# Four lower halves of an exponential table: from a product on VectorE to an exponential on ScalarE, in a new order

## The chip, the cores and the metric

The kernel runs on one core of a Trainium2 chip. The metric is the time of one execution on the device in microseconds (us), as the median of several runs. In all that follows PE is TensorE, PEld its weight loads, DVE is VectorE, ACT is ScalarE, POOL is GpSimd and SP is SyncE, which issues most of the DMAs.

## The reference

Two branches over the same input x (2048 positions, 512 channels) are mixed by a gate:

```python
g = _sigmoid((x * gate_w).sum(-1, keepdims=True))
a = _A_ref(x, ...)          # long convolution of each channel
b = _B_ref(x, wqkv, w_phi, wo)  # linear attention, 32 heads of 16
return g * a + (1 - g) * b
```

Branch A builds, for each channel d, a filter of 2048 lags from 128 complex states, and convolves by FFT:

```python
logdA = dt * A
P = jnp.exp(logdA[:, :, None] * l[None, None, :])
K = jnp.einsum("dn,dnl,dn->dl", Cc, P, dB).real
```

Branch B has features softmax(q w_phi) and softmax(-q w_phi), likewise for k, and divides num by den.

## The kernel before

**Units.** The 512 channels are cut into 16 units U of 32 channels; four units make a quarter Q. The filter of a unit is a sum over the 128 states (the partitions) of a coarse table A (32 steps of 64 lags) times a fine table R (64 lags). `plan_tables` makes the cosines and sines `cs` of the fine table (two Sin activations a unit), `plan_exp` its magnitudes `E`, `kgen` the rest. DVE makes A in two products A1, A2 (L1116, L1121), and for units whose digit in `FOURS` is 0 a sum A3 (L1126). It makes R in two products: `Rh` (L1133) from E's upper half and `Rl` (L1137) from E's lower half with `cs` read backwards. PE sums A times R into `kps`, which is copied out as `KD`.

**E.** A product of `statE` and `selE` on PE puts the 32x32 arguments of a unit (decay rate times lag t + 1/2, with t from 0 to 31) into a PSUM tile `args`. ACT's Exp gives the upper half, `E[:, 1]`. The lower half, `E[:, 0]`, has lags from -31.5 to -0.5. It is the upper half times exp(-32 x rate), kept in `Gtab`; DVE does that product, node `El`, L1063:

```python
nc.vector.tensor_tensor(out=T.E[:, 0]..., in0=T.E[:, 1]...,
                        in1=g.G[:, 32 * U:32 * U + 32].unsqueeze(2).to_broadcast([128, 32, 16, 2]), op=ALU.mult)
```

**Transforms.** `KD` goes through PE's stage `psA` (copied out as XA) and `psB` (copied out as XK, L143 on ACT, L145 on DVE). DVE multiplies XK by the input's transform, loaded as `XUX` (or into Dtab), giving `t` (L1251, and L1254 for the units 14 and 15). PE's `psz` turns back (copied out as Zr). For quarters 0 to 2 Zr goes to DRAM (`Zd`) and returns turned as `ZT`; for quarter 3 DVE turns it in place (L1337). PE's `psy` adds the attention to it, and DVE multiplies by the gate into xT (L1388, L1391). Units 14 and 15 go through this alone, unit 15 in halves.

**Attention.** Keys come first, up to about 75 us. Queries come in four blocks. In each, ACT exponentiates `pq` into Eq, `zs` sums it, and a short chain runs to and fro: ACT Ln (`zs`, `den`), DVE (L887 to L889), ACT Ln (`den`), DVE (L895), ACT Exp (`apm`). SP writes `apm` to DRAM (`apd`, L909) and reads it back spread over the partitions as `ax` (L916). DVE multiplies Eq by `ax` (L923, twice a block), then PE's `ops` makes the output, copied out as oT. There is one buffer for `ax`, which ZT uses too. The last block is the late one; its scaled copies are at L991 (ACT) and L993 (DVE), and the copies `Ctab<-psy` hold what the other quarters give it.

**Order.** Nothing is scheduled at run time. Every step is a node, `ORDER` lists all nodes in the order of issue, and each engine works off its own nodes in that order. `SIDES` says for each eviction whether ACT or DVE does it, `RINGS` which of two PSUM rings a tile comes from (each ring has two tiles of two banks), and `WARM` puts extra matmuls ahead of some. An engine whose next instruction waits holds up all that is behind it, SP's queue of DMAs included.

Of the kernel before, what the change touches and what calls it, by code (L numbers as in the profile page):

```python
# [10 lines left out]
ACT = mybir.ActivationFunctionType  # L11
# [58 lines left out]
class Plan:  # L70

    DIGITS = "0123456789abcdefghijklmnopqrstuvwxyzABCDEFGHIJKLMNOPQRSTUVWXYZ-_"
    ORDER = ("0H0J0B0C0D100L001112130y0z0A0102030j0k0l0m0n0o0d0e0f0g0h0i0405060s0t0u0a0b0c0708090p0q0r180I0T0U0V0W0K0M0X0O0P0Z0Q0R0Y0-0N14"
             "2u2w2x2v152Q2S2R2T2U2W16191a2V2Y2-2Z1x2_2y2z0S0_17342X1v2A1b1d1m1e1n1y1f1z2B2K2I2L1G2J301w3231331o1H1I0v0w0x2E2C2G2D2O2F1K2P"
             "1J1M1B1A35361D2H371E1c1p1q1r1g1h1i0E0F0G2M383a2N1C394B4I4K4J4L3c4X3d3b1F4P4Z4Y4-4M4_3e4T3g1X4N4U4Q4O4R4V52564S4W3h1Q571S3f5a"
             "5c3i53503j5b511T54585d5h4C5e554D593k3m5l1Y1U5i3l5f1L5g3n5m3Q5n5j5p5r5q5s3o3q3p3r5w5A5B1N5t5k5o3v3x5E3R5u5v5x5y5C1R5G5L3w3S5F"
             "5H5z5P3y5M1O4E1P3s3t3u3z3A3B3C3E5D5T5I5J5K5U5V5W5X5Q5N3D5R3F1V5-5O623J3L5S5Y3T5_3K5Z636064666768696a3U3V6d61656l6n3M6e3W3Y6m"
             "6o6p6b3G3H3I1s1t1u3N3O3P3X6q6c3Z6r3-3_6h406i6f426s41441W1Z1-261_436t20226j28456w4647486g4a2749294b2a6x2c6y2b216u232d2e2n244c"
             "4d4e4f4h6k6v4i4g4m4o2f2o4p4n2g6z2p4j4k4l2h2i2j2k2l254t4v4w2q4F2r2s2m4u4q4r4s4x4y4z1j1k1l2t4A8y6A6E9j9k9l6B6C6D9d9e9f8z8A6F8j"
             "6H8l8n8k8p8m8o8q8r4G8v8w4H9g9h9i6G6I8x8B8C6J8E8F8G8K8L6L8S7c8D6K6M6N8T7e7gag6O7d7hah8H8I8J6P8U8Y6Q7f6R8Z8M8N7i7L6S7j6T6U6V8s"  # L80
             "8t8u6W6X6Y6-6_708O8_907N7k8Q8P7l8V8W95918X7m7O7M7n8R96ai7o8-7Pap7R7Qaq7pa6aaab92936Zar94717q7r7s7t7u7v7x7y7z9798a7aca972aeam"
             "ajanak737wavawal999b749aa89cadaf7S76aoaD7T78aE9p7U77asat7A7V799q757W9r7XaFaJauaxay9xaM7B7D9yaN7Y9z9s9A7E9t7C9BaKc7c89FbZ7Z7-"
             "7_b1b2b38081828485869u9v9w9C9D9E9m9n9oaOaGaH9GaSaIc983879HaTc1c27Fb_7Gc47H9N9OazaB88aAaC897IaLc0c58a7Jb-8c8b7Kc3c68e7a8daPaQ"
             "cd9Pce8faRaU7baV8gcgaW8hch8icacbcccmcicn9IcDaXcE9QaY9JaZ9Ra-a_b0eEeFeGcRcScTeBeCeD9S9T9U9K9L9M9V9W9Xcfbacubbcvd-bie0d_bjcFcj"
             "ckcwclcJcKbcbke1eNcobdbleOcpbebme2bqbycAcBcxcye3bzbre4cz9_eWe5eXa0cqcse6a1cre7b4b5b6b7b8b99Y9Z9-bfbgbhe8e9eabnbobpdQcCcta2a3"
             "dRdUdVdWbsbAcGcHeYa4cIePeTeUa5cLcMbtbudScNcPbBcOcQd1d9cXcYcZebecedefegehcUcVcWbvbwbxbCbDbEbFd2eQeReeeid3f0daeSdbejeVekdXdhdi"
             "d4dpdqdcdTd5dddYdZeKeLeMbGbHbIc-c_d0bJbKbLf1eZe-dje_drd6d7d8dedfdgeHeIeJbMbNfmdkf2bOdsdlfndtdmdndoelf3embPfHbQf4f6fIdDfpfqfo"
             "fsftbRfrf7bSf5fuf8fvfbfwf9fxfcdudvdwdxdydzdAdBdCfJfNfOfKfLfMdEdGdHdIfafddFfyfzfAdJfPfQfRfSfTfUenfVfefheofWepfffifXfYfZfBfgfj"
             "f-f_fCg0fDg2eqg1fEg3dNdOdPdKdLdMbWbXbYbTbUbVereseteufkeyezeAevewexflfFfGg4g5g6g7g8g9gagb")
    SIDES = ("01110001001001010000000011000101001010000000110110000000100001100110010101011010000000000100000000000100000000000000"  # L90
             "0000000000000000000000000000100010000000000100000010110")
    RINGS = ("00001011111110101110000000000000000000101000000000000000001001000010000000101101000111110010111111011110001110101000"
             "00011001")
    WARM = ("01000000000001000050000200004000010000300000000060000004030050000010005000060100000040000310600000001000000030000000"
             "10000000000000000000100")
    FOURS = ("0111110101011000")
    ZPS = ("00000001")

    HOT = ("pk", "vp", "pq", "zp", "ops", "bps4", "psA", "psBu", "psB128", "psB64", "psB32", "psz", "pszn", "psyn32", "psy128", "psy64", "psy32", "kps")
# [47 lines left out]
    def run(self):  # L147
        code = {d: i for i, d in enumerate(self.DIGITS)}
        order = [64 * code[a] + code[b] for a, b in zip(self.ORDER[0::2], self.ORDER[1::2])] or list(range(len(self.nodes)))
        assert sorted(order) == list(range(len(self.nodes)))  # L150
        sides, rings, warm = iter(self.SIDES), iter(self.RINGS), iter(self.WARM)
        for n in self.nodes:
# [516 lines left out]
def attention_keys(P, nc, g, psum, r):  # L669
# [40 lines left out]
    for s2 in range(8):  # L710
# [20 lines left out]

        def ps4(K=K, box=box, on=P.ZPS[s2] == "1"):
            if not on:
                return
            box.ps = bank("zk")
            for u in range(2):
                e = K.E[:, u].rearrange("p g (h a b) -> p (g h) a b", a=4, b=4)
                for k in range(4):
                    nc.tensor.matmul(box.ps[:, 256 * u:256 * u + 256], lhsT=g.ident[:], rhs=e[:, :, k, :], start=(k == 0), stop=(k == 3), skip_group_check=True)

        def rd(K=K, box=box, on=P.ZPS[s2] == "1"):
            K.Z = g.kwk.tile([128, 2, 2, 32], F32, name="Zk")
# [302 lines left out]
def plan_exp(P, nc, g, psum, U, T, psq, deps):  # L1045

    act = g.act
    h, cc = U // 2, U % 2
    box = Bag()

    def pe():
        T.E = g.epool.tile([128, 2, 32, 32], BF16, name="E", bufs=g.P.k["E"])
        box.ps = psum([128, 2, 16, 32], "args")
        for e in range(2):
            nc.tensor.matmul(box.ps[:, e], lhsT=g.statE[64 * e:64 * e + 64, h, :], rhs=g.selE[64 * e:64 * e + 64, 16 * cc:16 * cc + 16, :],  # L1055
                             start=True, stop=True, tile_position=(64 * e, 0))

    def ex():
        act(out=T.E[:, 1], in_=box.ps[:].rearrange("p e x t -> p (e x) t"), func=ACT.Exp)
        box.ps = None  # L1060

    def el():
        nc.vector.tensor_tensor(out=T.E[:, 0].rearrange("p c (t k) -> p c t k", k=2), in0=T.E[:, 1].rearrange("p c (t k) -> p c t k", k=2),  # L1063
                                in1=g.G[:, 32 * U:32 * U + 32].unsqueeze(2).to_broadcast([128, 32, 16, 2]), op=ALU.mult)
    a = P.add("PE", "argE", pe, deps, take=[psq, "E"], rw=("stE selE", ""))
    T.nE.append(P.add("ACT", "E", ex, [a], drop=["psum"], tab="L"))
    T.nE.append(P.add("DVE", "El", el, T.nE[-1:], rw=("G", "")))


def plan_conv(P, nc, g, psum, r):  # L1070
# [33 lines left out]
    def kgen(units, XA, new, split=False):  # L1104
        K = Bag()
        K.done, kps, nu = [], [], len(units)
        for cc, U in enumerate(units):
            t = T[U]
            plan_exp(P, nc, g, psum, U, t, psq, [sh])
            four = P.FOURS[U] == "1"  # L1110
            c = Bag()
# [537 lines left out]
```

## Time and profile before

| | |
|---|---|
| runs | 251.51 us median of 3 (250.56 to 252.16) |
| the profiled execution | 251.85 us, its span 250.1 us |
| granted PE clock, mean | 0.977 |
| busy PE, PEld, DVE, ACT, POOL | 204.3, 140.2, 233.5, 222.0, 9.6 us |

The span runs from the first to the last instruction. Busy time of an engine is the sum over its instructions. In a timeline a row gives start, duration, engine, line, operation, tiles and shapes; what stands in brackets at its end is the time for which the engine had nothing running ahead of it, and what ended that. In a row of groups the count is followed by the total busy time, the mean duration in ns, and the idle time ahead.

### The profile page before, as it was taken

The numbers are of one execution on the slowest core, as the hardware profiler recorded it, in microseconds if no ns is written. First come the engines' busy times: TensorE is split into PE (matmuls) and PEld (weight loads), VectorE is DVE, ScalarE is ACT, GpSimd is POOL, SyncE is SP. The second block draws the span as 40 slices with busy tenths as digits, with TensorE's granted clock in tenths as the row PEclk, the third lists the DMA queues.
The fourth block names the chain that finished last, engine by engine and source line by source line (L and its number), as shares of the span: only waits on it lengthen the run. The fifth ranks groups of instructions, "written<-read, shape, count | busy, mean of one in ns | idle before, by whom it ended". The sixth has DMA issues, their size and how long they took to land.

```text
span 250.1 us, 9880 instructions
## 1 busy us (share of the span) xinstructions
PE 204.3 (82%) x4387; PEld 140.2 (56%) x4409; DVE 233.5 (93%) x316; ACT 222.0 (89%) x309; POOL 9.6 (4%) x21
## 2 busy tenths in 40 slices
PE   0687999999955846999897888999988698889980
PEld 0677566555634512556555645855767376677440
DVE  7999999999999999999979999999989799999890
ACT  7999999999999899999999899999989978875540
POOL 4820000000000000000000000000000000000000
PEclk9999999999999797999999999999999999999996
DMA  6998000445503765605350078554655979850645
GB/s 187 202 208 210 17 3 4 128 128 155 144 0 99 229 190 145 229 7 146 111 164 9 5 230 213 181 160 84 223 164 136 265 175 292 202 172 18 127 113 101
DMA packets 52842, 34.86 MB, mean 139 GB/s; under 512 B 30528, under 2 KB 48320, under 8 KB 52800
## 3 DMA queue, kind: packets, MB, share of 16 engines
q1 hardware_dynamic: 51456, 33.78, 51.4%
q8 instruction: 34, 0.56, 1.0%
q10 hardware_dynamic: 1344, 0.46, 0.9%
q14 instruction: 8, 0.07, 0.1%
HBM read 21.38 MB, written 12.58 MB: 136 GB/s over the span
## 4 chain that ended last, share of the span: by engine, by line
PE 29%; DVE 20%; DMA 19%; ACT 16%; issue 8%; SPq 5%; DVEq 0%; ACTq 0%
PE pk L718 5%; DMA ax<-apd 5%; PE vp L766 5%; DMA UD<-in_A_u_dram 4%; ACT cs L67 3%; DVE t L1251 2%; ACT Eq L67 2%; PE psz L1280 2%; PE kps L177 2%; DMA wc<-in_B_w_phi_dram 2%; DMA XUX<-XUd 2%; DVE R L1133 2%; DVE xT L1391 2%; DMA ZT<-Zd 2%; PE pq L852 2%
## 5 line engine op out<-in xcount | busy, mean ns | idle before, releaser
L177 PE MATMUL kps<-R,A 128*32 128x64 bf16 x1600 | 29.4, 229 | 1.8 <-DVE A L1121 1.8
L67 ACT ACTIVATE cs<-args 128x1024 bf16<-128x1024 f32 x32 | 30.7, 1052 | 0.0
L177 PEld LDWEIGHTS <-A 128*32 128x32 bf16 x1600 | 27.3, 161 | 5.7 <-DVE A L1121 2.2
L1116 DVE TENSOR_TENSOR A<-Ctab,Dtab 128x2048 bf16<-128x2048 bf16 x16 | 19.5, 1218 | 0.2 <-PE kps L177 0.2
L1133 DVE TENSOR_TENSOR R<-E,cs 128x2048 bf16<-128x2048 bf16 x16 | 19.5, 1219 | 0.0
L1137 DVE TENSOR_TENSOR R<-E,cs 128x2048 bf16<-128x2048 bf16 x16 | 19.5, 1218 | 0.0
L1121 DVE TENSOR_TENSOR A<-Ctab,Dtab 128x2048 bf16<-128x2048 bf16 x16 | 19.5, 1219 | 0.0
L143 ACT CAST Zr<-psz 128x1024 bf16<-128x1024 f32 (+1 forms) x16 | 16.0, 1026 | 3.7 <-DMA Zd<-Zr 1.9
L143 ACT CAST XA<-psA 128x1024 bf16<-128x1024 f32 (+1 forms) x17 | 16.5, 1005 | 1.6 <-PE psA L184 1.5
L67 ACT ACTIVATE Ek<-pk 128x512 bf16<-128x512 f32 x32 | 16.7, 604 | 0.7 <-PE pk L718 0.6
L67 ACT ACTIVATE E<-args 128x1024 bf16<-128x1024 f32 x16 | 16.9, 1053 | 0.4 <-PE args L1055 0.4
L67 ACT ACTIVATE Eq<-pq 128x512 bf16<-128x512 f32 (+1 forms) x28 | 16.8, 685 | 0.2 <-PE pq L852 0.2
L852 PE MATMUL pq<-xT,Wqp 128*128 128x512 bf16 x64 | 16.3, 386 | 0.4 <-ACT Eq L67 0.4
L745 DVE TENSOR_REDUCE Zk<-Ek 128x64 f32<-128x1024 bf16 x14 | 16.4, 1209 | 0.0
L766 PE MATMUL vp<-WW,xT 128*128 128x512 bf16 x62 | 15.9, 380 | 0.2
L718 PE MATMUL pk<-WW,xT 128*128 128x512 bf16 x58 | 14.5, 379 | 0.6 <-issue 0.5
L1251 DVE TENSOR_TENSOR t<-XUX,XK 128x2048 bf16<-128x2048 bf16 x12 | 14.5, 1219 | 0.3 <-DMA XUX<-XUd 0.3
L143 ACT CAST XK<-psB 128x1024 bf16<-128x1024 f32 (+1 forms) x14 | 13.7, 1000 | 1.0 <-PE psB L190 1.0
L625 PE MATMUL psB<-XAu,TB 64*128 64x128 bf16 x256 | 10.5, 231 | 4.5 <-ACT xst L143 2.5
L143 ACT CAST xst<-psB 128x1024 bf16<-128x1024 f32 x13 | 13.2, 1040 | 0.9 <-DMA XUd<-xst 0.9
L64 ACT ACT_TABLE_LOAD x10 | 12.8, 1283 | 0.9 <-PEq L1633 0.7
L923 DVE TENSOR_TENSOR Eq<-Eq,ax 128x2048 bf16<-128x2048 bf16 x8 | 9.7, 1221 | 4.0 <-DMA ax<-apd 4.0
(215 smaller groups left out, 504.8 us busy)
## 6 DMA issues: line engine op xcount, KB each, us to landing
XUX<-XUd SPq DMA_DIRECT2D x28, 256.0 KB, 4.4
XUd<-xst SPq DMA_DIRECT2D x8, 512.0 KB, 3.0
ax<-apd SPq DMA_DIRECT2D x16, 256.0 KB, 5.0
Zd<-Zr SPq DMA_DIRECT2D x24, 128.0 KB, 4.2
ZT<-Zd SPq DMA_DIRECT2D x6, 512.0 KB, 5.5
UD<-in_A_u_dram SPq DMA_DIRECT2D x16, 128.0 KB, 4.5
XUd<-xst SPq DMA_DIRECT2D x8, 256.0 KB, 3.7
wqk<-in_B_wqkv_dram SPq DMA_DIRECT2D x1, 1024.0 KB, 5.5
```

The costliest lines, as they stand in the source:

```text
L67: return self.nc.scalar.activation(**kw)
L143: self.nc.scalar.copy(out=o, in_=i)
L177: nc.tensor.matmul(kps[32 * dj:32 * dj + 32, g4, e, :], lhsT=A[:, ka, :, :, d].rearrange("p a b -> p (a b)"), rhs=R[:, kr, d, :], start=(i ...
L718: nc.tensor.matmul(box.ps[:], lhsT=xT[:, st, kt, :], rhs=g.WW[:, kt, :], start=(kt == 0), stop=(kt == 3))
L745: nc.vector.tensor_reduce(out=K.Z[:, u].rearrange("p g h -> p (g h)"), in_=K.E[:, u].rearrange("p g (h f) -> p (g h) f", f=16), axis=mybir ...
L766: nc.tensor.matmul(box.ps[:], lhsT=xT[:, st, kt, :], rhs=g.WW[:, 4 + kt, :], start=(kt == 0), stop=(kt == 3))
L852: nc.tensor.matmul(box.ps[:, m - m0, :] if late else box.ps[:], lhsT=g.Wqp[:, kt, 128 * m:128 * m + 128], rhs=xT[:, 4 * b:4 * b + 4, kt, : ...
L1116: nc.vector.tensor_tensor(out=c.A[:, 0:2].rearrange("p o a b c -> p (o a) b c"), in0=g.C[U // 8][:, 0:2, :, d0 % 256:d0 % 256 + 32].rearra ...
L1121: nc.vector.tensor_tensor(out=c.A[:, 2:4].rearrange("p o a b c -> p (o a) b c"), in0=g.C[U // 8][:, 1:3, :, d0 % 256:d0 % 256 + 32].rearra ...
L1133: nc.vector.tensor_tensor(out=c.R[:, :, :, 32:64], in0=t.E[:, 1].unsqueeze(1).to_broadcast([128, 2, 32, 32]), in1=t.cs[:], op=ALU.mult)
L1137: nc.vector.tensor_tensor(out=c.R[:, :, :, 0:32], in0=t.E[:, 0].unsqueeze(1).to_broadcast([128, 2, 32, 32]), in1=t.cs[:, ::-1, :, ::-1], o ...
L1251: nc.vector.tensor_tensor(out=box.t, in0=Ls[r0 // ns].X[:], in1=box.XK[:].unsqueeze(1).to_broadcast([128, 2, 1024]), op=ALU.mult)
```

## The change

For units 12 to 15 (`ELS`) ACT makes the lower half too, from the same PSUM arguments, with the sign turned by `scale=-1` and the lags written backwards; exp(-(t + 1/2) x rate) at the place 31 - t is what the product gave. The PSUM tile is released after the second exponential. DVE's El stays for units 0 to 11. `ORDER`, `SIDES`, `RINGS` and `WARM` are new throughout:

```diff
-    ORDER = ("0H0J0B0C0D100L001112130y0z0A0102030j0k0l0m0n0o0d0e0f0g0h0i0405060s0t0u0a0b0c0708090p0q0r180I0T0U0V0W0K0M0X0O0P0Z0Q0R0Y0-0N14"
...
+    ORDER = ("0H0J0L100B0C0D120y0z0A0d0e0f0j0k0l0m0n0o0405060102030g0h0i0s0t0u0a0b0c0p0q0r070809180I0T0011130X0V0U0Z0W0-0Y0K0M0N2w0O2u142v"
...
     FOURS = ("0111110101011000")
+    ELS = ("0000000000001111")
...
     def ex():
         act(out=T.E[:, 1], in_=box.ps[:].rearrange("p e x t -> p (e x) t"), func=ACT.Exp)
+        if not low:
+            box.ps = None
+
+    low = P.ELS[U] == "1"
+
+    def ela():
+        act(out=T.E[:, 0, :, ::-1], in_=box.ps[:].rearrange("p e x t -> p (e x) t"), func=ACT.Exp, scale=-1.0)
         box.ps = None
...
-    T.nE.append(P.add("ACT", "E", ex, [a], drop=["psum"], tab="L"))
-    T.nE.append(P.add("DVE", "El", el, T.nE[-1:], rw=("G", "")))
+    T.nE.append(P.add("ACT", "E", ex, [a], drop=([] if low else ["psum"]), tab="L"))
+    if low:
+        T.nE.append(P.add("ACT", "El", ela, [T.nE[-1], a], drop=["psum"], tab="L"))
+    else:
+        T.nE.append(P.add("DVE", "El", el, T.nE[-1:], rw=("G", "")))
```

The lines behind move: L1063 becomes L1071, and what stands behind plan_exp moves by 11, the copies by 1. Evictions change sides: counted over the order, after unit 0's first product DVE gets two casts of Ctab, two of oT, one large one of KD, a half of Zr, one scale (L993) and two casts of 256 columns (KD and xT), and gives up one large XK, one half XK and one cast of oT into wo. Ahead of it DVE gets one xst and one wT and gives up one XAu and one WW. ACT has the opposite of each.

Three places of the order. The first is on DVE, between the first and the second query block's Eq. Before:

```order
L923 TENSOR_TENSOR Eq<-Eq,ax 128x2048
L1133 TENSOR_TENSOR R<-E,cs 128x64x32
L1116 TENSOR_TENSOR A<-Ctab_75,Dtab 128x2048
L1137 TENSOR_TENSOR R<-E,cs 128x64x32
L1121 TENSOR_TENSOR A<-Ctab_75,Dtab 128x2048
L145 CAST wo<-ops 128x512
L923 TENSOR_TENSOR Eq<-Eq,ax 128x2048
L1133 TENSOR_TENSOR R<-E,cs 128x64x32
```

and in the change:

```order
L924 TENSOR_TENSOR Eq<-Eq,ax 128x2048 x2
L1127 TENSOR_TENSOR A<-Ctab_75,Dtab 128x2048
L1132 TENSOR_TENSOR A<-Ctab_75,Dtab 128x2048
L1144 TENSOR_TENSOR R<-E,cs 128x64x32
L146 CAST wo<-ops 128x512
L1148 TENSOR_TENSOR R<-E,cs 128x64x32
L1144 TENSOR_TENSOR R<-E,cs 128x64x32
L1148 TENSOR_TENSOR R<-E,cs 128x64x32
L924 TENSOR_TENSOR Eq<-Eq,ax 128x2048 x2
```

Six large operations and a cast stand between the blocks instead of four and a cast, and the two halves of a block follow each other at once. The second place is on ACT, in the last query block, from `zs` to `apm`. Before:

```order
L67 ACTIVATE zs<-zs 128x256
L67 ACTIVATE den<-zs 128x256
L143 CAST XK<-psB 128x1024 x2
L67 ACTIVATE den<-den,eps 128x128
L67 ACTIVATE E<-args 128x1024
L143 CAST XA<-psA 128x32x32
L67 ACTIVATE apm<-zs 128x256
```

and in the change:

```order
L67 ACTIVATE zs<-zs 128x256
L67 ACTIVATE den<-zs 128x256
L67 ACTIVATE E<-args 128x1024
L67 ACTIVATE E<-args 128x32x32
L144 CAST XK<-psB 128x1024 x2
L144 CAST XA<-psA 128x32x32
L67 ACTIVATE den<-den,eps 128x128
L144 CAST XA<-psA 128x32x32
L67 ACTIVATE apm<-zs 128x256
```

Unit 13's lower half (the form 128x32x32) and a second XA stand ahead of apm now, and the second `den` stands behind the first XA. The third place is DVE's end, from unit 15's A3 to its last t. Before:

```order
L1126 TENSOR_TENSOR A<-A 128x2048
L1388 TENSOR_TENSOR xT<-psy,gT 128x4x128
L1251 TENSOR_TENSOR t<-Dtab,XK 128x2048 x2
L1391 TENSOR_TENSOR xT<-psy,gT 128x2x4x128
L145 CAST XK<-psB 128x1024
L1254 TENSOR_TENSOR t<-XUX,XK 128x2x512
L145 CAST XK<-psB 128x512
L1254 TENSOR_TENSOR t<-XUX,XK 128x2x512 x3
```

and in the change:

```order
L1137 TENSOR_TENSOR A<-A 128x2048
L1262 TENSOR_TENSOR t<-Dtab,XK 128x2048
L1402 TENSOR_TENSOR xT<-psy,gT 128x2x4x128
L146 CAST KD<-kps 128x256
L1399 TENSOR_TENSOR xT<-psy,gT 128x4x128
L1262 TENSOR_TENSOR t<-Dtab,XK 128x2048
L1265 TENSOR_TENSOR t<-XUX,XK 128x2x512 x2
L146 CAST xT<-bps 128x2x128
L994 TENSOR_SCALAR xT<-bps,gT 128x384 x2
L1265 TENSOR_TENSOR t<-XUX,XK 128x2x512 x2
```

Both copies of XK have left DVE for ACT; a half of KD, a copy and a scale of the late block's output have come in.

More of the change, by code (lines that the diff above doesn't have):

```diff
@@ L72 @@
     DIGITS = "0123456789abcdefghijklmnopqrstuvwxyzABCDEFGHIJKLMNOPQRSTUVWXYZ-_"
-    ORDER = ("0H0J0B0C0D100L001112130y0z0A0102030j0k0l0m0n0o0d0e0f0g0h0i0405060s0t0u0a0b0c0708090p0q0r180I0T0U0V0W0K0M0X0O0P0Z0Q0R0Y0-0N14"
[L74 to L95, printed above, removed]
+    ORDER = ("0H0J0L100B0C0D120y0z0A0d0e0f0j0k0l0m0n0o0405060102030g0h0i0s0t0u0a0b0c0p0q0r070809180I0T0011130X0V0U0Z0W0-0Y0K0M0N2w0O2u142v"
+             "150P162x2y0Q0R191a2Q2S2T2R2U2W2V2z2X2Y2-2Z2_1x0_0S17341b1d1m1e1n1f2A1v1o1y1z2K1G1H1I1c0v0w0x2B2L35362I30322J2G1w2H1A1B1D371E"
+             "33312C2E2D2F2O2M1p1q1r0E0F0G1s1t1u383a2N2P4B1N3b391X1C4I4K4J4L3c4X4Z4Y4-3d4M3e4P4T3f4N4O4Q4U4R4V4_523g1R3h564S3i50531O573j51"
+             "1F4W3k3l54585a5c3m5b5d5h5l55594C5p5e1Y1L1S5i3n1J3Q5f5g3R4D5m5n5j5q4E3o5r5s3q3p3r5w5x1T5A5t5B1K3v5k5o5u5v3s3t3u8s8t8u1g1h1i3w"
+             "5y5C5E5G5F5H5L5M1P3x3y3C5P5z5D3E5I5T5V3D5Q5J5K3z3A3B3F4F5R5N3S5U5W3J3L5-625O5S5X5Y3M5_3K1U3T635Z606466671Q68693U6a6d61651M1V"
+             "6l6n3V3W3Y6m6o6p6e6b3X3N3O3P6q3Z6c6r6f6h3-403_6s421W1Z1-43411_26206i216j2223446w46452747282c6g484a6x6y2a292b244b492d2e3G3H3I"
+             "4f4h4g2f4i4c4d4e1j1k1l4j4k4l4m4o2n2g2o6t2h2i4n4p2p2q6u2j256k4q4r4s2r2k2l2m2s2t4t4v4w4u4x4y4z4A6F6v8k8o6H6z8j8l6A8y8z6E9g9h9i"
+             "8n8p8m8q8r4G8v7c8w6I8E4H8A8x8B8C7d8F8G8K8L8S6J6L8D6G6K6M7e6N8T7f6O7Lag7g7i7Mah8H8I8Y8J8U6P7j6Q8Z6R7h6S6T6U6V6W6X6Y6-6_708M7N"
+             "8_7k8N8O907P8Q8P7Q7lai8V8W8X9195967m8R7O7n8-ap7R927oaq7pa6aaab9394ar6Z717q7r7s6B6C6D9j9k9l7t7u7v7x7y7z9d9e9f9798a772a974acae"
+             "ajakam73anavaw7wal7A999b9a9ca876aoadaf7SaDaE7T789p7U779q7975asataJ7V7WauaF9r7XaKaxay9xaM7B9yc77D7YaNc87C9z9s9A9t9BbZ9F7Z7-7_"
+             "9m9n9o808182848586aGaSaHaO9G7Fb_7Hc1c2c4aI7I83aT87c97G9N9OazaB88aAaC897EaLc0c58a8c8eb-8b8daPaQcd9H9P8faRaUc3c6aV7acg7Jch7baW"
+             "aX7Kcecacbcicccmcn8gcD8h8icEeBeCeDa-a_b09C9D9E9u9v9weEeFeG9I9Jb4b5b6b1b2b3aY9QaZcf9R9S9T9U9K9L9M9V9W9Xcubacvbbd-bie0d_bjcFcj"
+             "ckcJclcKeNbcbkcocpcwcAcBe1eOePbdeWblbebmb7b8b99Y9Z9-eKeLeMbnbobpbfbgbhe2bqe3eXeYbr9_bybza0cqcscxcye4czcre5a1e6cte7cCdQa2a3dR"
+             "dUdVbscGcHa4a5bAcIeTbtdWbucLcMbBbCe8e9eacRcScTebecedefegehcUcVcWbDbEbFbvbwbxcNcPcOdScQd1d9dXd2daeQeUeReSeeeif0d3dbejekeVdhdp"
+             "did4dqdTdcd5dYdddZbGbHbIcXcYcZc-c_d0d6d7d8bJbKbLdedfdgeZf1e-e_djbMbNfmbOdrdkf2dsfndlfodtf3bPfHfIfJelf4bQf6fsfpftfqfrbRbSf5eH"
+             "eIeJdmdndodudvdwdxdydzdAdBdCfufKfNfLfOfMdDfvemf7fwfxf8fbf9fadEdGfcfyfPdHdFfzfQfRfSdIdJfdfAfBenfTfUfVfWfXeoepeqfYfZfefhfffifg"
+             "fjf-fCf_fDg0g1g2g3fEdNdOdPdKdLdMbTbUbVbWbXbYereseteueyezeAfkevewexflg4g5fFfGg6g7g8g9gagb")
@@ new lines @@
+    SIDES = ("01110001001011000000000010100010011001000000110110000000100011100100100111001000000110000100000000000100010000000000"
+             "0000100100000000000000000011100001000000000000100001110")
+    RINGS = ("00011011111111001010000000000000000000001000000000000000101001000010000000101100010111110100101111011010000100111000"
+             "01010010")
+    WARM = ("00000000100110000020000500001000060000300004000000000006003024110100036000060201000021000010200000000000000000002003"
+             "01000002000000000000000")
```

## The prediction

> **What bounds the kernel now.** I read the totals of the page first, then busy time in stretches of 10 us, then the timelines of VectorE (DVE), ScalarE (ACT) and TensorE (PE), then the chain of waits.
>
> ```profile
> PE 204.3 (82%) x4387; PEld 140.2 (56%) x4409; DVE 233.5 (93%) x316; ACT 222.0 (89%) x309; POOL 9.6 (4%) x21
> ...
> PE 29%; DVE 20%; DMA 19%; ACT 16%; issue 8%; SPq 5%; DVEq 0%; ACTq 0%
> ```
>
> DVE is the fullest engine, and no engine holds a third of the chain: the end is set by hand-overs. The average hides where ACT is free, so the stretches (us, then PE, PEld, DVE, ACT, POOL busy):
>
> ```profile
> 30.00:40.00 10.00, 9.91 (x231) 6.92 (x232) 9.78 (x13) 9.85 (x20) 0.00 (x0) 1.00 0.02 4
> ...
> 90.00:100.00 10.00, 5.45 (x32) 1.67 (x30) 9.66 (x18) 9.97 (x12) 0.00 (x0) 0.83 0.63 175
> 100.00:110.00 10.00, 9.29 (x264) 5.91 (x263) 9.97 (x13) 9.91 (x20) 0.00 (x0) 1.00 0.44 146
> ...
> 180.00:190.00 10.00, 8.84 (x262) 7.61 (x250) 9.31 (x12) 8.84 (x13) 0.00 (x0) 1.00 0.54 163
> 190.00:200.00 10.00, 7.29 (x192) 4.99 (x189) 8.20 (x9) 10.00 (x12) 0.00 (x0) 1.00 0.89 231
> ...
> 210.00:220.00 10.00, 8.53 (x218) 6.54 (x219) 9.74 (x11) 8.09 (x10) 0.00 (x0) 1.00 0.89 227
> 220.00:230.00 10.00, 9.14 (x329) 8.19 (x328) 9.66 (x10) 6.01 (x10) 0.00 (x0) 1.00 0.34 111
> ```
>
> Up to 180 us DVE and ACT are both full. At 190 to 200 ACT is full and DVE waits. From 210 on ACT is free and DVE is full. Units 14 and 15 fall into the free part, units 12 and 13 into the full one. All that is left to win on DVE after 100 us is its idle time, in the brackets of its timeline:
>
> ```profile
> 131.06 1.23 DVE L923 TENSOR_TENSOR Eq<-Eq,ax 128x2048 bf16<-128x2048 bf16 x1 [1.63 <-DMA ax<-apd]
> ...
> 185.34 1.23 DVE L1391 TENSOR_TENSOR xT<-psy,gT 128x1024 bf16<-128x1024 f32 x1 [0.65 <-PE psy L1378]
> ...
> 199.25 1.23 DVE L923 TENSOR_TENSOR Eq<-Eq,ax 128x2048 bf16<-128x2048 bf16 x1 [1.80 <-DMA ax<-apd]
> 201.00 1.23 DVE L923 TENSOR_TENSOR Eq<-Eq,ax 128x2048 bf16<-128x2048 bf16 x1 [0.52 <-DMA ax<-apd]
> ...
> 234.36 0.69 DVE L145 CAST XK<-psB 128x512 bf16<-128x512 f32 x1 [0.90 <-ACT XK L143]
> ```
>
> **What leaves DVE and what comes to it.** The rows by form give durations:
>
> ```profile
> L1063 DVE TENSOR_TENSOR E<-E,Gtab 128x1024 bf16<-128x1024 bf16 x16 | 11.0, 685 | 0.1
> L67 ACT ACTIVATE E<-args 128x1024 bf16<-128x1024 f32 x16 | 16.9, 1053 | 0.4 <-PE args L1055 0.4
> L1137 DVE TENSOR_TENSOR R<-E,cs 128x2048 bf16<-128x2048 bf16 x16 | 19.5, 1218 | 0.0
> L1133 DVE TENSOR_TENSOR R<-E,cs 128x2048 bf16<-128x2048 bf16 x16 | 19.5, 1219 | 0.0
> L145 DVE CAST XK<-psB 128x1024 bf16<-128x1024 f32 x2 | 2.4, 1216 | 0.0
> L145 DVE CAST wo<-ops 128x512 bf16<-128x512 f32 x2 | 1.4, 683 | 0.0
> L993 DVE TENSOR_SCALAR xT<-bps,gT 128x384 bf16<-128x384 f32 x1 | 0.5, 549 | 0.0
> L143 ACT CAST KD<-kps 128x1024 bf16<-128x1024 f32 x7 | 7.3, 1042 | 0.1
> L143 ACT CAST Ctab<-psy 128x512 bf16<-128x512 f32 x3 | 1.9, 626 | 1.9 <-DVE xT L1388 1.9
> ```
>
> Back to back, neighbours overlap, so an instruction takes a slot shorter than its duration:
>
> ```profile
> 102.52 0.69 DVE L1063 TENSOR_TENSOR E<-E,Gtab 128x1024 bf16<-128x1024 bf16 x1
> 103.13 1.22 DVE L1133 TENSOR_TENSOR R<-E,cs 128x2048 bf16<-128x2048 bf16 x1
> 104.26 1.22 DVE L1137 TENSOR_TENSOR R<-E,cs 128x2048 bf16<-128x2048 bf16 x1
> ...
> 98.49 1.02 ACT L67 ACTIVATE E<-args 128x1024 bf16<-128x1024 f32 x1
> 99.41 2.06 ACT L67 ACTIVATE Eq<-pq 128x512 bf16<-128x512 f32 x4
> ```
>
> 103.13 less 102.52 is 0.61 us for a lower half; 104.26 less 103.13 is 1.13 us for a large operation; 99.41 less 98.49 is 0.92 us for an exponential. Four lower halves leave DVE: 4 x 0.61 = 2.44 us. Four exponentials come to ACT: 4 x 0.92 = 3.68 us.
>
> The new instruction writes its lags backwards, and no ACT row of before does. Lower bound: the forward row, 0.92 us. Upper bound: half rate, 1.84 us. On DVE the product that reads backwards (L1137, 1218 ns) costs what the forward one does (L1133, 1219 ns); that is the nearest row, so I take 0.92 us. It also holds its two PSUM banks one exponential longer; each PSUM ring has two tiles, so I count that within the ranges below.
>
> The order moves evictions too, and this is what I weigh most. After 100 us DVE gets two Ctab casts and two oT casts (4 x 0.60 = 2.4), one large KD cast (1.13), one Zr half (0.60), one L993 scale (0.47) and two casts of 256 columns (about 0.3 each, an estimate from the 549 ns row): 5.2 us. It gives up one large XK (1.13), one XK half (0.60) and one wo cast (0.60): 2.33 us. With the lower halves the sum is 5.2 - 2.33 - 2.44 = **+0.4 us**: DVE has no less to do after 100 us. Before that it gives up WW and one XAu and takes one xst and one wT: 0.60 - 1.13 = -0.5 us. ACT is the mirror: +3.68 less about 2.7 of casts after 100 us (the same ones, at its own 0.5 to 0.95 us slots), level before. So the gain can come only from waits.
>
> One rule speaks against such a move: the Trainium skill, "ScalarE: Activation LUTs", Rules for kernel authors, sends plain multiplies to VectorE as the faster engine for them. The trace agrees (685 ns against 1053 ns), and by that rule the change costs engine time wherever ACT is full.
>
> **Term 1, preparation up to unit 0's first product (99.7 us).** DVE loses 0.5 us of work and ACT is level; at 30 to 40 us PE is the fullest engine, and less work on DVE gains nothing there. Bounds: -0.5, and +0.5 if the new order waits as much more. I take -0.3.
>
> **Term 2, up to the last query block.** In the second block's Eq the 1.63 us are a wait for a DMA that cannot start before the first block's Eq has freed the only ax buffer:
>
> ```profile
> 122.95 1.22 DVE L923 TENSOR_TENSOR Eq<-Eq,ax 128x2048 bf16<-128x2048 bf16 x1
> ...
> 125.22 4.06 SPq L916 DMA_DIRECT2D ax<-apd  x4
> ```
>
> Before, four large slots and a cast (5.1 us) stand between the two Eq; now six and a cast (6 x 1.13 + 0.60 = 7.4 us). That covers the first half's 1.63 us. But the second half's Eq follows at once now, and its two loads were issued some 2 us behind the first two, so I let 0.6 us of wait come back: -1.0. Against it stand the KD cast and the extra oT work before 185 us: 1.13 + 0.60 = +1.73, of which the 0.65 us that DVE waited for psy there take their part. Together +0.2 (bounds -1.6 and +1.7).
>
> **Term 3, the last query block.** The rows are ACT's, then SP's and the DMA's:
>
> ```profile
> 183.36 0.42 ACT L67 ACTIVATE den<-den,eps 128x128 f32<-128x128 f32 x1
> ...
> 185.91 1.01 ACT L143 CAST XA<-psA 128x1024 bf16<-128x1024 f32 x1 [1.03 <-PE psA L184]
> 186.81 0.39 ACT L67 ACTIVATE apm<-zs 128x256 bf16<-128x256 f32 x1
> ```
> ```profile
> 192.01 2.48 SPq L916 DMA_DIRECT2D ax<-apd  x4
> ```
> ```profile
> 193.89 7.01 DMA ax<-apd
> ```
>
> Now den stands behind the first XA, which waits for psA until 185.91: den ends near 187.1, DVE's zs (queued behind it: t, A, A and all the rest) waits some 0.6 us, and apm comes behind the second XA, near 188.1 instead of 186.81. SP sends apm out, then an XUX load, then ax; before, ax issued 5 us after apm began, held also by the XUX load and by psy having freed the buffer. Of the 1.3 us I let 0.3 through (bounds 0 and 1.3). DVE has 10.3 us of slots between zs and Eq where it had 12.0, which only lengthens the wait there. Term: +0.3.
>
> **Term 4, the tail.** From the last Eq on, DVE has one large slot (XK) and two lower halves less and small casts more: -0.65 us. The XK half that waited 0.90 us for ACT is on ACT now, and three scales and casts fill the gap ahead of unit 15's t. So unit 15's t ends up to 1.6 us earlier. But PE limits what comes of it:
>
> ```profile
> 225.08 0.47 PE L1378 MATMUL psy<-ZT,TF 64*32 64x128 bf16 x32 [0.66 <-DMA ZT<-Zd]
> ...
> 235.71 0.39 PE L1316 MATMUL psz<-t,TI 128*128 128x512 bf16 x1 [0.26 <-ACT Zr L143]
> 236.31 1.46 PE L1316 MATMUL psz<-t,TI 128*128 128x512 bf16 x6 [0.21 <-DVE t L1254]
> ...
> 239.87 0.89 PE L1371 MATMUL psy<-xT,ident 128*128 128x512 bf16 x2
> ```
>
> Between 225.08 and 239.87 these are PE's idle times, 0.47 us, and 0.66 us lie ahead of them. Bounds: -1.13 and 0. I take -1.0, near the full idle time, because ACT, busy 6.01 of 10 us there, no longer holds anything up. Units 14 and 15's exponentials cost nothing: ACT's idle time covers them; without that cover they would add 1.84 us.
>
> **Sum.** -0.3 + 0.2 + 0.3 - 1.0 = -0.8 us. The profiled execution took 251.85 us (span 250.1); 251.05 after. The median of the runs shown, 251.51, lies 0.34 below it: **250.7 us**, with its own range 249.0 to 252.6.
>
> **Rivals.**
> *The waits go.* The new order removes the two ax waits (1.63, 1.80 + 0.52) and the tail's 0.90, and takes 0.5 in preparation: -5.35 + 0.4 + 0.5 for what psy still holds gives -4.4, or 251.51 - 4.4 = 247.1 us. For it: all are order effects, and the order is new. Against it: both ax loads start on an event (buffer free, apm) that the change does not make earlier.
> *ACT becomes the bound in the last query block.* Place: ACT from 171 to 188 us. Units 12 and 13's exponentials (1.84 us) and the XA ahead of apm (0.9) enter there, the KD cast (0.95) leaves; with den's wait apm comes 2.2 us later. It decides once apm ends so late that ax, not the XUX load ahead of it, is what SP waits for: from then each us goes one to one into Eq, where DVE waits already, and PE's ops behind it. With the tail no better and +0.4 of term 2: 251.51 + 2.2 + 0.4 = 254.1 us. For it: ACT is at 10.00 of 10 at 190 to 200. Against it: its 1.03 us wait for psA absorbs part. By the Trainium skill's rule on multiplies, given above, this would be the case to expect.
> *The change does not do what it says:* a backward write at half rate adds 4 x 0.92 = 3.7 us to ACT, half of it in the full part: 252.5 us, inside the first range.
>
> **How the numbers follow.** A measurement of this kernel can tell 1%, 2.5 us, from no change. Forecast and half-rate case: 0.53, all within 1%. Waits go: 0.27, faster. ACT bound: 0.20, slower. The range reaches most of the way to both: 247.6 to 254.0 us.
>
> **What would show it.** Right: the four ACT forms at about 1.05 us; 12 lower halves on DVE; DVE busy within 1 us of 233.5; ACT about 223; Eq of the last block still waiting 1 us or more for ax; the last t before 236 us. Wrong: DVE idle under 3 us between 100 and 240 (the first rival), apm after 189 us with Eq past 201 (the second), or ACT's new form near 1.9 us. A preparation that ends more than 1 us away from 99.7 would break the sum in a place that I priced only by bounds.

## The result, and the profile after

The changed kernel takes 254.72 us (median of 4 runs, 254.42 to 255.90), the kernel before in the same comparison 251.80 us: ratio 1.0134, 95% interval 1.0096 to 1.0172. It is slower by 1.3%, where I forecast 0.3% faster, and it lies outside my range. The profiled execution took 254.98 us, its span 253.1 us. The totals and the chain's shares, from the page of the changed kernel:

```profile
PE 208.8 (83%) x4392; PEld 141.5 (56%) x4415; DVE 233.8 (92%) x318; ACT 223.7 (88%) x307; POOL 7.8 (3%) x21
...
DVE 26%; PE 22%; ACT 21%; DMA 18%; issue 7%; SPq 3%; ACTq 0%; DVEq 0%; POOL 0%; POOLq 0%
```

DVE and ACT have the work that I counted (233.5 and 222.0 us before), so most of the 3 us must be waits. The exponentials and the lower halves, from the groups by form of the changed kernel:

```profile
L67 ACT ACTIVATE E<-args 128x1024 bf16<-128x1024 f32 x20 | 20.4, 1047 | 0.1
...
L1071 DVE TENSOR_TENSOR E<-E,Gtab 128x1024 bf16<-128x1024 bf16 x12 | 8.2, 686 | 0.4 <-ACT E L67 0.4
```

Sixteen of the twenty write forwards and four backwards. Their mean, 1047 ns, is below the 1053 ns of before, so a backward write costs what a forward one does. Now the same places in both DVE timelines, by the start of the instruction unless the row says end. Each timeline is one execution, and executions of one preparation differ by some tenths of a us (a pair of runs below shows 0.8), so only the large steps count:

| place on DVE | before | after | delay | my sum said, up to here |
|---|---|---|---|---|
| unit 0's first lower half | 99.66 | 103.31 | +3.65 | -0.3 |
| next after the last block's Eq | 202.14 | 205.12 | +2.98 | +0.2 |
| end of the last t | 236.86 | 239.45 | +2.59 | -0.8 |
| end of the last xT | 243.98 | 247.13 | +3.15 | -0.8 |

The whole loss is there before unit 0's first product. The stretches there, of after (us, then PE, PEld, DVE, ACT, POOL busy, granted clock):

```profile
80.00:90.00 10.00, 6.07 (x133) 4.37 (x134) 9.93 (x18) 7.91 (x9) 0.00 (x0) 0.66 0.78 221
90.00:100.00 10.00, 5.42 (x56) 1.66 (x59) 7.60 (x14) 8.49 (x10) 0.00 (x0) 0.51 0.60 173
100.00:110.00 10.00, 9.93 (x149) 4.38 (x142) 8.52 (x9) 9.97 (x17) 0.00 (x0) 0.81 0.01 2
```

At 90 to 100 us DVE was busy 9.66 and ACT 9.97 us before; now 7.60 and 8.49. Read backwards from there, the DVE timeline of after names what it waits for:

```profile
94.75 0.17 DVE L798 TENSOR_TENSOR zj<-kvp,mask 128x16 f32<-128x16 f32 x1 [1.51 <-PE kvp L784]
...
101.10 0.69 DVE L704 TENSOR_SCALAR zrow<-zps 128x512 f32<-128x512 f32 x1 [1.82 <-PE zps L699]
...
103.31 0.69 DVE L1071 TENSOR_TENSOR E<-E,Gtab 128x1024 bf16<-128x1024 bf16 x1 [0.38 <-ACT E L67]
```

PE's kvp and zps stand in PE's queue behind the `args` products of the cosines, and these need PSUM that ACT must empty:

```profile
91.69 0.79 PE L1034 MATMUL args<-selE,statC 64*128 64x512 bf16 x2 [3.23 <-ACT xst L144]
```

The ACT timeline of after shows where ACT stood:

```profile
84.92 1.09 ACT L144 CAST xst<-psB 128x1024 bf16<-128x1024 f32 x1
85.83 2.09 ACT L67 ACTIVATE trg<-pb 128x1024 bf16<-128x1024 int16 x2
90.63 1.93 ACT L144 CAST xst<-psB 128x1024 bf16<-128x1024 f32 x2 [2.72 <-DMA XUd<-xst]
92.52 1.94 ACT L67 ACTIVATE cs<-args 128x1024 bf16<-128x1024 f32 x2
95.33 5.60 ACT L67 ACTIVATE cs<-args 128x1024 bf16<-128x1024 f32 x6 [0.88 <-PE args L1034]
100.96 1.28 ACT L64 ACT_TABLE_LOAD   x1
```

and the same place in the ACT timeline of before:

```profile
86.97 1.01 ACT L143 CAST xst<-psB 128x1024 bf16<-128x1024 f32 x1 [0.88 <-DMA XUd<-xst]
87.88 1.06 ACT L67 ACTIVATE trg<-pb 128x1024 bf16<-128x1024 f32 x1
88.84 1.00 ACT L143 CAST xst<-psB 128x1024 bf16<-128x1024 f32 x1
89.73 7.45 ACT L67 ACTIVATE cs<-args 128x1024 bf16<-128x1024 f32 x8
```

Before, the eight `cs` ran unbroken; now they begin 2.79 us later and break. The xst casts fill two buffers in turn; a cast waits until the store of its buffer (to XUd, in DRAM) has landed. The stores are SP's, and this is SP's queue after:

```profile
51.67 28.34 SPq L638 DMA_DIRECT2D XUd<-xst  x8
80.06 4.86 SPq L369 DMA_DIRECT2D statE<-pz  x8
85.05 8.54 SPq L638 DMA_DIRECT2D XUd<-xst  x6
```

and before:

```profile
62.90 27.96 SPq L637 DMA_DIRECT2D XUd<-xst  x10
90.90 4.91 SPq L368 DMA_DIRECT2D statE<-pz  x8
```

The eight loads of `statE` (the arguments' left side) stood behind the last store; the new order puts them ahead of the last three stores, two pieces each. For 4.86 us no store can be issued, but only the end of that counts: the sixth store's casts were done at 83.66 us (82.60 and 1.06), and it is issued at 85.05, 1.4 us late. My prediction did not look at SP in this stretch.

### The profile page after: what moved, and what is told of

Its sections match the earlier page's. It is cut to its first block, busy times and chain, and to the rows that moved or that the text cites. A ratio compares the mean times of both kernels' runs of the same rounds, so it can differ in the third digit from the quotient of the medians.

```text
span 253.1 us, 9886 instructions
## 1 busy us (share of the span) xinstructions
PE 208.8 (83%) x4392; PEld 141.5 (56%) x4415; DVE 233.8 (92%) x318; ACT 223.7 (88%) x307; POOL 7.8 (3%) x21
## 4 chain that ended last, share of the span: by engine, by line
DVE 26%; PE 22%; ACT 21%; DMA 18%; issue 7%; SPq 3%; ACTq 0%; DVEq 0%; POOL 0%; POOLq 0%
DMA ax<-apd 6%; DMA XUd<-xst 5%; PE pq L853 4%; DVE t L1262 4%; ACT cs L67 3%; PE pk L719 3%; DMA XUX<-XUd 2%; ACT xst L144 2%; PE vp L767 2%; DMA Zd<-Zr 2%; DVE A L1127 2%; DVE R L1148 2%; ACT XA L144 2%; ACT xT L144 2%; DVE A L1132 2%
## 5 line engine op out<-in xcount | busy, mean ns | idle before, releaser
L67 ACT ACTIVATE E<-args 128x1024 bf16<-128x1024 f32 x20 | 20.4, 1047 | 0.1
L144 ACT CAST XK<-psB 128x1024 bf16<-128x1024 f32 (+1 forms) x16 | 15.0, 970 | 3.5 <-DVE t L1262 2.0
L853 PE MATMUL pq<-xT,Wqp 128*128 128x512 bf16 x64 | 17.5, 411 | 0.0
L144 ACT CAST Zr<-psz 128x1024 bf16<-128x1024 f32 x15 | 15.4, 1041 | 2.0 <-DMA Zd<-Zr 0.9
L144 ACT CAST xst<-psB 128x1024 bf16<-128x1024 f32 x12 | 12.1, 1040 | 3.2 <-DMA XUd<-xst 2.7
L1291 PE MATMUL psz<-t,TI 128*128 128x512 bf16 x42 | 11.9, 380 | 3.1 <-DVE t L1262 1.3
L626 PEld LDWEIGHTS <-TB 64*128 64x128 bf16 x256 | 8.8, 105 | 9.3 <-issue 8.8
```

What stands on the lines that cost most here:

```text
L67: return self.nc.scalar.activation(**kw)
L144: self.nc.scalar.copy(out=o, in_=i)
L626: nc.tensor.matmul(box.ps[:, c2, sl, :], lhsT=fc.TB[rows, b0:b0 + 2].rearrange("p a b -> p (a b)"), rhs=X.t[rows, k, r0 + sl].rearrange("p ...
L853: nc.tensor.matmul(box.ps[:, m - m0, :] if late else box.ps[:], lhsT=g.Wqp[:, kt, 128 * m:128 * m + 128], rhs=xT[:, 4 * b:4 * b + 4, kt, : ...
```

## The experiments

**Theory:** those eight issues ahead of the stores hold ACT's xst casts, and with them cs, PE and DVE. **Rivals:** the new order on DVE there (the KVbd products, node `kvbd`, stand ahead of the first A product, so DVE waits for kvp); the four exponentials on ACT; the lower granted clock as a cause. In the diffs two characters of `ORDER` are a node: `1j1k1l` is the statE load (issue, transfer, landing), `4c4d4e`, `4j4k4l`, `4q4r4s` and `4x4y4z` are the last four XUd stores, `3G3H3I` the store ahead of them.

### statE late

```diff
-"...4c4d4e1j1k1l4j4k4l..."
+"...4c4d4e4j4k4l..."
-"...2s2t4t4v4w4u4x4y4z4A..."
+"...2s4t4v4w4u4x4y4z1j1k1l2t4A..."
```

(`2t` only releases buffers that the load's source used; it follows the load.)

> The changed kernel with one edit: the eight statE loads are issued behind the last XUd store instead of between the stores; all else is as changed. Theory (the loads in SP's queue held the stores, and these held ScalarE's xst casts): no wait of more than 1 us of ACT's xst for XUd<-xst, the first product of unit 0 at 99.5 to 101 us instead of 103.3, the whole at 251.2 to 252.8 us. Rival 'VectorE's order' (kvbd ahead of the first A product): the product stays at 102 us or later, the whole above 253.5. Rival 'the four exponentials on ScalarE cost it': no change, 254.3 to 255.2.

Measured: 251.76 us, ratio to before 1.0011 (0.9971 to 1.0051). SP, ACT and DVE of this run:

```profile
90.81 1.00 SPq L638 DMA_DIRECT2D XUd<-xst  x2
91.86 5.20 SPq L369 DMA_DIRECT2D statE<-pz  x8
```
```profile
88.86 1.93 ACT L144 CAST xst<-psB 128x1024 bf16<-128x1024 f32 x2 [0.33 <-issue]
90.67 7.46 ACT L67 ACTIVATE cs<-args 128x1024 bf16<-128x1024 f32 x8
```
```profile
100.50 0.69 DVE L1071 TENSOR_TENSOR E<-E,Gtab 128x1024 bf16<-128x1024 bf16 x1 [0.35 <-ACT E L67]
```

The wait of 2.72 us is down to 0.33, cs runs unbroken, the product comes 2.81 us earlier, and the time falls by 2.96 us. DVE's order is unchanged here and its waits for kvp and zps are gone too: they were passed on, and the first rival falls. The clock falls as a cause (last section). What is left of the change, with these loads late, cannot be told from no change; the 0.3% that I forecast lies at the edge of the interval.

The chains of waits of the changed kernel and of this run put sizes to it. They show the sixth store, from the issue of its second piece to the landing:

```profile
85.47 5.10 DMA XUd<-xst
```
```profile
84.70 3.82 DMA XUd<-xst
```

Besides the 1.4 us for which it was held, the store took 1.3 us longer to land; together about the 2.72 us of the cast's wait. In the changed kernel the seventh store is issued 0.7 us behind that piece (86.16 us), here 2.0 us behind it (86.65), so that two stores moving at once are the likely reason; no run tests that. The break in cs, 0.88 us, comes on top.

### The kernel before with statE early

```diff
-"...4c4d4e4f4h..."
+"...4c4d4e1j1k1l4f4h..."
-"...4x4y4z1j1k1l2t4A..."
+"...4x4y4z2t4A..."
```

> The kernel before with one edit: its eight statE loads are issued between the fifth and the sixth XUd store, where the changed kernel has them. Theory: the later stores come up to 4.9 us later, ACT's xst waits 2 us or more for them, the first product of unit 0 at 101.5 to 103.5 us instead of 99.7, the whole at 253.3 to 255.3 us. Both rivals (VectorE's order, the four exponentials): nothing here changes, 251.3 to 252.2 us.

Measured: 255.33 us, ratio 1.0137 (1.0063 to 1.0211), by its middle value the whole loss of the change without the change. Its ACT and DVE:

```profile
90.33 1.01 ACT L143 CAST xst<-psB 128x1024 bf16<-128x1024 f32 x1 [3.98 <-DMA XUd<-xst]
```
```profile
103.39 0.69 DVE L1063 TENSOR_TENSOR E<-E,Gtab 128x1024 bf16<-128x1024 bf16 x1 [1.51 <-ACT E L67]
```

### statE elsewhere: at once, and in a gap

The first of two runs issues the loads right behind the write that they read (`1i` is its landing), the second behind the fourth store; both take them away from their place behind `4e`:

```diff
-"...1g1h1i3w5y..."
+"...1g1h1i1j1k1l3w5y..."
```
```diff
-"...3G3H3I4f4h..."
+"...3G3H3I1j1k1l4f4h..."
```

> The changed kernel with one edit: the eight statE loads are issued right behind the write of pz that they read, at about 52 us, where SP then waits some 17 us for casts anyway. Same loads, same queue, a place with slack. Theory (what cost the time is the 4.9 us of issue between two stores that ScalarE waits for): the first product of unit 0 at 99.5 to 101 us, the whole at 250.8 to 252.6 us. Rival 'it matters only that statE comes after the stores, or the order on VectorE': 253.5 us or more.

> The changed kernel with one edit: the eight statE loads are issued behind the fourth XUd store, near 60 us, where no cast of xst runs between 59 and 77 us and so no store is ready to issue. The run with the loads at 53.6 us held the second store and made ScalarE's xst wait 6.9 us; the theory (the issue counts where it stands ahead of a store whose buffer ScalarE waits for) says that here nothing waits: no ACT xst wait above 1 us, first product of unit 0 at 99.5 to 101 us, 250.8 to 252.6 us. Rival 'the loads must come after all stores': 253.5 us or more.

At once: 258.08 us, ratio 1.0249 (1.0196 to 1.0302): my expectation failed, though the mechanism did not. I had read the row `51.67 28.34 SPq` as one wait; it is four stores with waits between them, and the first of the four was ready at once. This run's SP, ACT and DVE:

```profile
53.57 5.02 SPq L369 DMA_DIRECT2D statE<-pz  x8
58.70 39.83 SPq L638 DMA_DIRECT2D XUd<-xst  x14
```
```profile
62.89 1.01 ACT L144 CAST xst<-psB 128x1024 bf16<-128x1024 f32 x1 [6.87 <-DMA XUd<-xst]
```
```profile
66.40 1.29 DVE L776 TENSOR_TENSOR vr<-vb,vr 128x1024 bf16<-128x1024 bf16 x2 [7.16 <-ACT vr L67]
```

The store waited behind the loads (and, with them, some 2 us for the landing of pz), the cast for the store, DVE for ACT. In the gap, where no cast of xst runs from 59 to 77 us, the same loads cost nothing: 252.03 us, ratio 0.9996 (0.9953 to 1.0040).

```profile
62.39 5.71 SPq L369 DMA_DIRECT2D statE<-pz  x8
79.13 12.34 SPq L638 DMA_DIRECT2D XUd<-xst  x8
```
```profile
100.15 0.69 DVE L1071 TENSOR_TENSOR E<-E,Gtab 128x1024 bf16<-128x1024 bf16 x1 [0.38 <-ACT E L67]
```

The same loads at 54, 62, 80 and 92 us give 258.1, 252.0, 254.7 and 251.8 us: not early or late, but what stands ready behind them decides.

### The exponentials in the order of before

Three runs take the order of before, with the four ACT lower halves directly behind their upper ones (`eP`, `eY`, `fo`, `fJ` behind `eO`, `eX`, `fn`, `fI`; the casts as before), all four, or those of two units:

```diff
+    ELS = ("0000000000001111")
...
+    ELS = ("0000000000000011")
...
+    ELS = ("0000000000001100")
```

> The kernel before with the four lower halves of units 12 to 15 made by ScalarE, each directly behind its upper half; everything else stands in the order of before. Theory: the preparation is untouched (first product at 99.7 us), and the whole is 251.2 to 252.6 us. Rival 'the four exponentials cost it': apm comes 1.8 us later or more in the last query block, 253.5 to 255 us.

> The kernel before with the lower halves of units 14 and 15 alone made by ScalarE, directly behind the upper ones. Theory from the run with all four (TensorE waited 0.71 and 1.21 us for ScalarE's E at 217 and 222 us, then VectorE's A 1.74 us for kps): the loss sits here, 252.8 to 254.5 us. Rival 'it sits at units 12 and 13, in the late ax of the last query block': 251.0 to 252.3 us, since ScalarE is idle for four of ten us at 220 to 230.

> The kernel before with the lower halves of units 12 and 13 alone made by ScalarE. With all four it was 3.4 us slower, with those of 14 and 15 alone 1.4. Theory (two separate costs that add up: here apm comes 0.6 us later behind ScalarE's longer queue, and Eq waits for ax): 252.6 to 254.5 us. Rival 'the loss is all at units 14 and 15': 251.2 to 252.3 us.

Measured: all four 255.14 us, ratio 1.0163 (1.0080 to 1.0246); units 14 and 15 alone 253.24 us, 1.0051 (1.0016 to 1.0086); units 12 and 13 alone 253.03 us, 1.0054 (1.0019 to 1.0088). My expectation for the first failed: by themselves the exponentials do cost, at both places (the two parts add up to 1.0105, inside the interval of the whole). With all four, PE waits 0.71 and 1.21 us for E ahead of psy, and behind it DVE waits for PE:

```profile
225.76 1.23 DVE L1127 TENSOR_TENSOR A<-Ctab,Dtab 128x2048 bf16<-128x2048 bf16 x1 [1.74 <-PE kps L178]
```

with those of 14 and 15 alone, PE:

```profile
217.41 0.38 PE L834 MATMUL psy<-wo,oT 128*128 128x128 bf16 x4 [0.61 <-ACT E L67]
...
222.00 0.38 PE L834 MATMUL psy<-wo 128*128 128x128 bf16 x4 [1.21 <-ACT E L67]
```

and before, at the second place:

```profile
219.26 0.38 PE L833 MATMUL psy<-wo 128*128 128x128 bf16 x4 [0.29 <-ACT E L67]
```

The wait of 1.21 us is 0.92 more than before, one exponential's slot. These products do not read E, so what they wait for must be the PSUM tile that the arguments of E held. ACT is free on average there, but not at this place: before, it runs without a gap from 213.60 to 221.52 us and is idle for 1.89 us ahead of that and 1.40 us behind it, and PE's next step waits for just these two. Whether the PSUM tile or ACT's queue counts more was not told apart. With units 12 and 13 alone the other place shows on DVE, before with 1.80 and 0.52 us:

```profile
200.79 1.23 DVE L924 TENSOR_TENSOR Eq<-Eq,ax 128x2048 bf16<-128x2048 bf16 x1 [4.03 <-DMA ax<-apd]
202.83 1.23 DVE L924 TENSOR_TENSOR Eq<-Eq,ax 128x2048 bf16<-128x2048 bf16 x1 [0.81 <-DMA ax<-apd]
```

### The new order without the exponentials

```diff
-    ELS = ("0000000000001111")
+    ELS = ("0000000000000000")
```

once in the changed kernel as it stands, and once with statE late and each lower half directly ahead of its reader on DVE:

> The changed kernel's order with the four lower halves back on VectorE at their places in it. Theory: the first product of unit 0 still at 103.3 us and the whole at 254 to 256 us. Rival 'the four exponentials cost it': 251 to 253 us.

> The changed kernel with statE late, and its four lower halves of units 12 to 15 back on VectorE, each directly ahead of the product that reads it (so that VectorE does not wait for it, as it did for 3.6 us in the run without the exponentials). It prices the four ScalarE exponentials in the new order, whose casts were moved to VectorE. Theory (the new order is made for them): VectorE has 4 x 0.61 us more, and most of it comes through: 252.8 to 254.5 us against 251.8 with them. Rival 'the exponentials are a cost in any order': 251.2 us or less.

The first took 263.11 us, ratio 1.0451 (1.0393 to 1.0508), far above what I expected, and says little of their worth: the products stand where ACT's exponentials stood, so DVE waits for the upper half at once, as its timeline shows:

```profile
223.99 0.69 DVE L1071 TENSOR_TENSOR E<-E,Gtab 128x1024 bf16<-128x1024 bf16 x1 [3.64 <-ACT E L67]
```

But its first product of unit 0 stands at 103.39 us, as expected: the loss ahead of it is there without the exponentials too.

The second took 253.96 us, ratio 1.0076 (1.0046 to 1.0106), against 251.76 with the exponentials. In the new order the exponentials are worth 2.2 us by the medians (1.6 by the two ratios, each of which is uncertain by 0.3 to 0.4%), near the 2.44 us of DVE slots that I counted; the same order without them is some 2 us slower than before. The casts that went from ACT to DVE would be their price, but no run moves the casts alone, and no order was made for the kernel without exponentials.

### A version below both

In the changed kernel the wo load and two XUX loads are issued around the ax loads of the second query block; in these runs they stand early (`6B6C6D` is wo, the others XUX), once with statE late, once with statE in the gap:

```diff
-"...9g9h9i8n8p..."
+"...9g9h9i9j9k9l6B6C6D9d9e9f8n8p..."
-"...7s6B6C6D9j9k9l7t7u7v7x7y7z9d9e9f97..."
+"...7s7t7u7v7x7y7z97..."
```

> The changed kernel with statE late, and in addition the wo load and two XUX loads issued early, behind the first XUX load as in the kernel before, instead of around the ax loads of the second query block. Theory: those ax loads land in 5.8 us or so instead of 7.9, Eq's waits of 1.40 and 0.66 us in that block fall below 1 us together, and the whole is 249.8 to 251.2 us. Rival 'the waits are handed on to the next block's ax': 251.3 to 252.2 us.

> As the run before (statE in the gap near 60 us), with the wo load and two XUX loads early as well. Theory: SP is done with the stores some 5 us sooner, the first product of unit 0 is no earlier than 100 us since VectorE is full before it, and no ax wait is left in the second query block: 250.2 to 251.8 us, at or a little below both kernels. Rival 'waits are handed on': as with statE late, 251.5 to 252.5 us.

With statE late alone, that block had this on DVE:

```profile
134.35 1.22 DVE L924 TENSOR_TENSOR Eq<-Eq,ax 128x2048 bf16<-128x2048 bf16 x1 [1.40 <-DMA ax<-apd]
136.24 1.22 DVE L924 TENSOR_TENSOR Eq<-Eq,ax 128x2048 bf16<-128x2048 bf16 x1 [0.66 <-DMA ax<-apd]
```

With the loads early both waits are gone, but the time is 251.51 us, ratio 0.9986 (0.9955 to 1.0018), no different from before: the last block, where DVE had waited 0.40 us in all, now shows

```profile
198.56 1.23 DVE L924 TENSOR_TENSOR Eq<-Eq,ax 128x2048 bf16<-128x2048 bf16 x1 [0.91 <-DMA ax<-apd]
200.54 1.23 DVE L924 TENSOR_TENSOR Eq<-Eq,ax 128x2048 bf16<-128x2048 bf16 x1 [0.75 <-DMA ax<-apd]
```

so that 1.26 of the 2.06 us came back there. In its profile DVE is still 1.43 us earlier behind the last Eq than with statE late alone, while the medians differ by only 0.25 us: what these loads are worth by themselves is not told. With statE in the gap as well: 250.29 us, ratio 0.9951 (0.9919 to 0.9982). That is below both kernels, by half a per cent of before; its one profile (span 250.2 us) is of its slowest execution (251.97 us) and no shorter than that of before, so where the half per cent comes from stays open.

## Why the prediction was wrong, point by point

**The step that failed is term 1, "preparation up to unit 0's first product".** It was priced at -0.3 with bounds of 0.5 either way, from DVE's and ACT's work alone; it measured +3.65 us. I costed the casts that moved and not the DMAs, though SP's rows of the kernel before show the statE loads and the new `ORDER` has them ahead of stores. Of the 3.65 us, 2.81 are the place of these loads (103.31 to 100.50 us). The 0.84 that are left are no more than executions differ by: with statE late and no exponentials, the same preparation ended at 99.70 us, level with before. My line that a preparation more than 1 us off would break the sum was the right guard, with nothing behind it.

**Terms 2 and 3** (+0.2 and +0.3) measured -0.67 together (3.65 to 2.98): DVE, 3.65 us late at that point, met ax loads of the last block that had mostly landed and waited less. With statE late, where it is not late, they came to +0.13 (0.84 to 0.97 us: 203.11 against 202.14 us behind the last Eq), within 0.4 us of the forecast, but that is largely luck, for two errors cancel. Term 2 let 0.6 us of wait stand in the second block, and DVE waits 1.60 and 0.81 us there (1.40 and 0.66 with statE late). In the changed kernel the ax loads are issued amid the wo and XUX loads, and from their issue to Eq it takes 8.35 us (128.49 to 136.84) where before it took 5.84 (125.22 to 131.06). Term 3 in turn had the waits of the last block grow, and with statE late they shrank from 2.32 to 0.40 us.

**Term 4** (-1.0) measured +0.17. With statE late the stretch to the last t was indeed 1.07 us shorter (+0.97 to -0.10), and in the changed kernel 0.39 shorter, with waits of 0.64 us for XUX and 0.73 for kps in the place of the 0.90 us that left. But behind the last t the changed kernel takes 0.56 us longer, and there stands a row of two Zr casts where before had one:

```profile
239.56 1.99 DVE L1348 STREAM_TRANSPOSE ZT<-Zr 128x512 f32<-128x512 f32 x2
241.64 1.29 DVE L146 CAST Zr<-psz 128x512 bf16<-128x512 f32 x2
242.85 1.90 DVE L1348 STREAM_TRANSPOSE ZT<-Zr 128x256 f32<-128x256 f32 x3
```

I had counted that half of Zr (0.60 us) in the sum over DVE, without asking where it stands. But the scale of 0.48 us that stood in this stretch before (239.01 to 239.49) now stands ahead of the last t, so the two nearly cancel. The other 0.4 us are in small gaps and overlaps (0.11 us between the last t and the first transpose, where before these overlapped by 0.09); no run takes them apart.

**The exponentials.** Their price on ACT, 0.92 us a slot, held (1047 ns mean against 1053). That units 14 and 15 "cost nothing: ACT's idle time covers them" failed as an argument: in the order of before the two cost 1.3 us (ratio 1.0051), with new waits of PE at two places where ACT had no gap, though it was idle for four of ten us in the stretch that I read. In the new order four of them are worth some 2 us on DVE; that the casts had made room for them is my reading.

**The second rival** (ACT bound in the last query block, 254.1 us) has about the right time for the wrong place, by luck. Its marks came true, apm at 191.43 and Eq past 201 us, but DVE was 3.65 us late from unit 0's first product on. With statE late apm is still 2.3 us later than the first product's delay explains (189.95 against 186.81 us, less 0.84), as that rival said, and Eq hardly waits: DVE has that much more to do in front of it. The first rival's waits did go in part and were replaced.

The Trainium skill, "DMA: Bandwidth & Descriptors", Rules for kernel authors, tells one to issue a DMA early and to wait on its semaphore late. Here the runs disagree for one place: the loads that moved to 80 us cost 3 us, since a store stood behind them; moved to 62 us, they cost nothing and gained nothing (252.03 us). The same page (Anatomy of one DMA — SWDGE (gpsimd) path) says that a DMA's wait is taken on the issuing sequencer before dispatch; the traces agree for SP, whose 4.86 us of loads hold up stores and whose waiting stores hold up what stands behind.

## What to carry over

When an order is made anew, compare each queue's own list, SP's above all, and for every DMA that moved ahead of another ask which buffer the other one frees and who waits for it. An empty stretch of a queue is slack only if nothing that stands behind it becomes ready in it, and a long row of several DMAs hides where that is. What such loads cost is not their whole length but the time for which the next DMA was ready (1.4 of 4.86 us here) and what follows from it. An engine that is idle for four of ten us can still cost its neighbours one for one (0.92 us for 0.92 us) where the next step waits for just the instruction that was added, and a term for "work moved" needs the place at which the work is put.

## What was not expected of the hardware

Eight loads of 32 KB hold SP for 4.86 to 5.71 us. In the changed kernel the first two take 0.95 and 1.10 us of it and the other six 0.47 us each, and at least for those issued after 83 us the transfers are not what takes the time: in this row (busy share of the 16 DMA engines in tenths, 40 slices of 0.25 us from 80 to 90 us) the engines are one to four tenths busy from 83 to 86 us, while from 83.66 us a store waits to be issued.

```profile
DMA  9999999999961324232332339999999998889999
```

The granted PE clock is not what cost the time here: with statE at 62 us it was 0.54 at 80 to 90 us, lower than the changed kernel's 0.66, with no loss of time:

```profile
80.00:90.00 10.00, 8.20 (x149) 5.18 (x145) 9.93 (x18) 9.50 (x12) 0.00 (x0) 0.54 0.80 232
```
